# Folding a two-tile chunk into the steps of a wide chunk, with the token weights moved by another queue

## The chip, the core and the metric

One core of a Trainium2 chip runs the whole kernel. The metric is the device time of one execution in microseconds (us). Its engines are TensorE (PE in the views, with its weight loads as PEld), VectorE (DVE), ScalarE (ACT), GpSimd (POOL) and SyncE (SP), which only issues DMAs here.

## The reference

Sliding-window attention over 4 sequences of 576 tokens with 8 heads of 64, then a block that mixes tokens and then channels, then a normalised channel block. All in float32, 2304 tokens of width 512:

```python
x = attention(q, k, v)                             # window of 128, a slope for each head
h = np.maximum(x.T @ w_tok1, 0) @ w_tok2           # mixing over the 576 tokens of a sequence
u = x + h.T
u = u + np.maximum(u @ w_ch1, 0) @ w_ch2           # "layer 0": 512 -> 1536 -> 512
xn = (u - mean) / sqrt(var + 1e-6) * g_ln
out = u + np.maximum(xn @ w_ch1b, 0) @ w_ch2b      # "layer 1": 512 -> 2048 -> 512
```

## The kernel before

The 2304 tokens are 18 tiles of 128. Attention and token mixing take about the first 160 us and run in one stream of tiles; then come the two channel layers. Each float32 operand is split in a high and a low float32r part, and a product is three matmuls (high by high, high by low, low by high). The high part is a copy on ScalarE (`copy`, L385), the low part a subtraction (`minus`, L401 on VectorE, or two halves of 256 columns on GpSimd, L403).

In a channel layer the tokens go in three chunks: tiles 0 to 7 (wide, c = 0), tiles 16 and 17 (small, c = 1), and tiles 8 to 15 (wide, c = 2). In each chunk a step handles two blocks of 128 hidden channels: 6 steps to a chunk in layer 0, 8 in layer 1, so 42 steps in all. A wide step makes the first product by a scheme of seven products of half size (`seven_products`, L1122), each of 6 matmuls of 512 columns, from seven prepared forms of the transposed tokens (`prep_wide`, L902: transposes, sums, splits) and seven forms of the weights (`w1_of`, L975, through a ring of four split places, `W1_BUFS`). A small step (`two_blocks`, L1223) makes two plain blocks of 12 matmuls of 256 columns from tokens that `prep_small` (L946) has prepared. Between the products stand the units of the step before: `second` (L1236) multiplies the hidden values of a tile by the second weights, 6 matmuls of 512 columns, and VectorE adds the result to the tile (L1256). In layer 1's last chunk a faster form of it is used in all steps but the last (`second_fast`, L1261).

The prepared forms of a wide chunk lie in one place each, so the next chunk's can only be written when the present chunk's last step has read them. In the kernel before, the forms of chunk 2 are prepared piece by piece during the steps of the small chunk, and those of the next layer's chunk 0 all in the last step of chunk 2.

Weights come as float64 and are turned to float32 on the chip (`load_f64`, L411: two loads of 512 KB, one ScalarE and four VectorE operations for a tile of 256 KB). Those of layer 1 are turned ahead of need and stored in DRAM (`stage_w`, L538); how many in each step says `STAGE_RATES`. Split second weights are stored too in chunk 0 and read back by the other chunks (`w2_of`, L1037).

The first token weights are needed a second time, shifted by 64 rows, for sequences 1 and 3: `shift_wt1` (L583) copies them within SBUF by six DMAs that GpSimd issues.

The order of work on each engine is not written by hand: `Plan` (L122) records each operation with a cost, what it reads and writes, and a due time that follows from the place of TensorE's operations in the program, and schedules the list greedily. A place in a ring comes free when the planned users of its last holder are done. The engines then run that order, waiting on semaphores. SP's DMA queue is one stream in that order too.

Of the kernel before, what the change touches and what calls it, by code (L numbers as in the profile page):

```python
# [24 lines left out]
P = 128  # L25
# [17 lines left out]
W1_BUFS, W2_BUFS, ST_BUFS, H_BUFS = 4, 4, 6, 6  # L43
X_SHIFT, STAGE_SHIFT, W1_SHIFT = -20, -20, -80

STAGE_RATES = {(0, 2): 2, (1, 0): 2}
# [291 lines left out]
def block_kernel(tc, qT, kT, v, wt1, wt2, wa1, wa2, wb1, wb2, g, bias, out):  # L338
# [150 lines left out]
    for layer in range(2):  # L489
        for c, tiles in enumerate((range(8), (16, 17), range(8, 16))):  # L490
            steps += [(layer, c, tiles, n) for n in range((NF1, NF2)[layer] // 2)]
# [410 lines left out]
    def prep_wide(layer, tiles):  # L902
# [39 lines left out]
        if layer == 0 and tiles[0] == 0:  # L942
            return xs, itertools.chain(*zip(pieces(0), pieces(1)))
        return xs, itertools.chain(pieces(0), pieces(1))

    def prep_small(layer, tiles):  # L946

        out = []
        sh, sl = few()
        for j in range(2):  # L950
            b = turned(layer, [(i, 2 * j + k) for k in range(2) for i in tiles])
            copy((sh, j), lambda j=j: sh.t[:, j, :CW], b, lambda b=b: b.t, CW, ("ACT",), True)
            minus((sl, j), lambda j=j: sl.t[:, j, :CW], b, lambda b=b: b.t, (sh, j),
                  lambda j=j: sh.t[:, j, :CW].bitcast(F32), CW, ("DVE",))
# [20 lines left out]
    def w1_of(s, ahead=None):  # L975

        f1, f2 = take_w(), take_w()
        if len(steps[s][2]) == 2:
            out = [w_split("w1", W1_BUFS, x) for x in (f1, f2)]
            keep_taken(2)  # L980
            return out
# [32 lines left out]
        def others(w0, w1):  # L1014
            w2 = w_split("w1", W1_BUFS, b, all_of(b))
            w3 = w_split("w1", W1_BUFS, f2, right(f2), HW)
            keep_taken(2)
            return [(w0, 0), (w1, 0), (w2, 0), (w1, HW), (w0, HW), (w3, 0), (w2, HW)]
# [103 lines left out]
    def seven_products(ws, xs, keep, end, hid, fast):  # L1122
# [42 lines left out]
        yield  # L1165
        product(5, bb, False, end)
        out(1, 0, bb)
        yield
# [54 lines left out]
    def two_blocks(ws, xs, hid):  # L1223

        hid[0] = hidden()
        for j, (wh, wl) in enumerate(ws):
            ps = bank(2 * j)
            for k, (sh, sl, h, c) in enumerate(xs):
                s = slice(k * P, (k + 1) * P)
                mm3(ps, lambda ps=ps: ps.t[:, :HW], wh, lambda s=s, wh=wh: wh.t[:, s], wl, lambda s=s, wl=wl: wl.t[:, s],  # L1230
                    (sh, h), lambda h=h, c=c: sh.t[:, h, c], (sl, h), lambda h=h, c=c: sl.t[:, h, c],
                    HW, k == 0, k == 3)
            relu_to(hid[0], j, slice(j * HW, (j + 1) * HW), ps, lambda ps=ps: ps.t[:, :HW], HW)
            yield

    def second(s, w2, hid):  # L1236

        layer, _, tiles, n = steps[s]
        turns = list(enumerate(tiles))
        if s == len(steps) - 1:  # L1240
            turns = turns[CT:] + turns[:CT]
        for t, i in turns:
            o = buf("pst", [P, DM], F32, "tok", 2)
            if len(tiles) == 2:
                hs = [(*hid[0], j, j * HW + t * P) for j in range(2)]
# [136 lines left out]
    for _ in pieces:  # L1382
        pass

# [14 lines left out]
    for s in range(len(steps) + 1):  # L1399
# [7 lines left out]
        if len(tiles) == 2:  # L1407
            parts, ns = two_blocks(w1, xs, hid), (4, 4)
        else:
            parts = seven_products(w1, xs, keep, s == len(steps) - 1, hid, fast2(s))  # L1410
            ns = (6, 8, 0, 0) if before and fast2(before[0]) else (2, 3, 3, 0)
# [5 lines left out]
        if before and n == 0 and layer + c > 0:  # L1417
            if steps[s - 1][0] == 0:
                todo.extend((tile_stats, i) for i in steps[s - 1][2])
                todo.append((chunk_stats, steps[s - 1][2]))  # L1420
# [73 lines left out]
```

## Time and profile before

| what | value |
|---|---|
| median of 3 runs | 833.73 us (833.47 to 835.28) |
| the profiled execution | 835.53 us |
| its span, first to last instruction | 833.8 us |
| TensorE busy | 821.5 us, 4732 matmuls |
| VectorE, ScalarE, GpSimd busy | 659.1, 428.5, 466.9 us |
| moved by DMA | 179.21 MB, mean 215 GB/s |
| granted TensorE clock, mean | 0.997 of full speed |

Busy times are shares of the span in which an engine has an instruction in it. A matmul's row is longer than its turn: one of 512 columns is listed with about 390 ns, while the next starts about 227 ns later. So a short stall of TensorE leaves no idle time in the table, and the distance between starts must be read.

### The profile page before, as it was taken

To read this page: it belongs to the slowest core of one execution; us is meant where nothing else is said; L and a number is where in the kernel's file an instruction comes from. 1 tells how busy PE (TensorE), PEld (TensorE's weight loads), DVE (VectorE), ACT (ScalarE), POOL (GpSimd) and SP (SyncE) were. 2 spreads that over 40 slices of the span, in tenths; PEclk is the share of its full clock that TensorE was granted. 3 is DMA by queue.
4 is the path that set the end of the run, shared out by engine and by line. 5 is a ranking of instruction groups with operands and counts; after the bars stand their busy time and mean duration, and the time that the engine had idled before them with its cause. 6 is when DMAs were issued, how large, how long until landed. Compare 5 with 4: busy or idle time off the path is not lost.

```text
span 833.8 us, 14352 instructions
## 1 busy us (share of the span) xinstructions
PE 821.5 (99%) x4732; PEld 693.4 (83%) x4732; DVE 659.1 (79%) x1379; ACT 428.5 (51%) x1015; POOL 466.9 (56%) x723
## 2 busy tenths in 40 slices
PE   8999999999999999999999999999999999999998
PEld 6777788888888898888888888888889889999996
DVE  5888777978787989987889868989666767777785
ACT  5888677643344535334368333447456634444430
POOL 2785466756354567544248666857533656666640
PEclk9999999999999999999999999999999999999999
DMA  9679645454678899987861544888977663443302
GB/s 328 191 184 306 232 140 191 143 186 144 216 226 297 293 317 322 339 293 240 280 238 54 188 154 139 290 309 300 354 263 237 226 226 130 137 141 116 102 26 101
DMA packets 80474, 179.21 MB, mean 215 GB/s; under 512 B 9104, under 2 KB 10768, under 8 KB 80400
## 3 DMA queue, kind: packets, MB, share of 16 engines
q1 hardware_dynamic: 79920, 176.98, 62.9%
q0 software_dynamic: 480, 1.31, 0.7%
q8 instruction: 37, 0.61, 0.3%
q14 instruction: 37, 0.30, 0.1%
HBM read 138.15 MB, written 38.80 MB: 212 GB/s over the span
## 4 chain that ended last, share of the span: by engine, by line
PE 92%; DVE 4%; ACT 3%; DMA 1%; issue 1%; POOL 0%; DVEq 0%; ACTq 0%; POOLq 0%
PE tok L1253 10%; PE tok L1251 10%; PE b L1138 10%; PE tok L1252 10%; PE b L1139 10%; PE b L1140 10%; PE tok L1288 5%; PE p L1288 4%; PE ps_s L636 3%; PE ps_v L648 3%; PE p L891 2%; PE b L482 2%; PE b L481 2%; PE b L480 2%; PE ps_t L693 1%; ACT pr L686 1%
## 5 line engine op out<-in xcount | busy, mean ns | idle before, releaser
L1256 DVE TENSOR_TENSOR u<-tok,u 128x512 f32<-128x512 f32 x196 | 134.4, 687 | 52.5 <-PE tok L1253 51.1
L1251 PE MATMUL tok<-w2h,hh 128*128 128x512 f32 x392 | 154.0, 393 | 0.0
L1253 PE MATMUL tok<-w2h,hl 128*128 128x512 f32 x392 | 152.9, 390 | 0.2 <-DVE hl L971 0.2
L1252 PE MATMUL tok<-w2l,hh 128*128 128x512 f32 x392 | 152.8, 390 | 0.0
L1138 PE MATMUL b<-xh,w1h 128*128 128x512 f32 x384 | 150.4, 392 | 0.3 <-DVE b L401 0.3
L1139 PE MATMUL b<-xl,w1h 128*128 128x512 f32 x384 | 149.8, 390 | 0.0
L1140 PE MATMUL b<-xh,w1l 128*128 128x512 f32 x384 | 149.6, 389 | 0.0
L403 POOL TENSOR_TENSOR w1l<-w,w1h 128x256 fp32r<-128x256 f32 (+1 forms) x112 | 78.9, 726 | 111.4 <-ACT w1h L385 103.4
L969 ACT ACTIVATE hh<-b 128x512 fp32r<-128x512 f32 (+1 forms) x112 | 58.7, 542 | 136.8 <-PE b L1140 95.5
L1253 PEld LDWEIGHTS tok<-w2h,hl 128*128 128x128 f32 x392 | 73.6, 188 | 16.4 <-DVE hl L971 0.8
L1251 PEld LDWEIGHTS tok<-w2h,hh 128*128 128x128 f32 x392 | 73.7, 188 | 15.1 <-DVE u L1256 0.8
L971 DVE SCALAR_TENSOR_TENSOR hl<-b,hh 128x512 fp32r<-128x512 f32 (+1 forms) x112 | 67.2, 617 | 23.9 <-ACT hh L969 23.2
L1252 PEld LDWEIGHTS tok<-w2l,hh 128*128 128x128 f32 x392 | 73.7, 188 | 14.3
L1140 PEld LDWEIGHTS b<-xh,w1l 128*128 128x128 f32 x384 | 72.1, 188 | 15.4
L1138 PEld LDWEIGHTS b<-xh,w1h 128*128 128x128 f32 x384 | 72.2, 188 | 14.6 <-DVE b L401 0.7
L1139 PEld LDWEIGHTS b<-xl,w1h 128*128 128x128 f32 x384 | 72.2, 188 | 13.5
L449 ACT ACTIVATE e<-rh 128x512 bf16<-128x512 bf16 (+2 forms) x62 | 39.7, 641 | 69.4 <-DMA rh<-wb 22.2
L403 POOL TENSOR_TENSOR w1l<-st,w1h 128x256 fp32r<-128x256 f32 x58 | 44.9, 795 | 47.9 <-ACT w1h L385 42.0
L686 ACT ACTIVATE pr<-t,mn 128x128 f32<-128x128 f32 x144 | 55.8, 391 | 14.1 <-DVE mn L677 14.0
L704 POOL TENSOR_SCALAR_AFFINE_SELECT pf<-pf 128x512 f32<-128x512 f32 x64 | 42.1, 659 | 34.6 <-ACT pf L385 28.3
L401 DVE TENSOR_TENSOR b<-b,p 128x512 f32<-128x512 f32 x56 | 38.9, 695 | 20.1 <-PE b L1140 19.5
L403 POOL TENSOR_TENSOR xl<-st,xh 128x256 fp32r<-128x256 f32 x48 | 39.0, 834 | 21.0 <-ACT xh L385 16.6
(193 smaller groups left out, 1919.9 us busy)
## 6 DMA issues: line engine op xcount, KB each, us to landing
w<-d SPq DMA_DIRECT2D x86, 256.0 KB, 4.2
rw<-wb SPq DMA_DIRECT2D x32, 512.0 KB, 5.4
rh<-wb SPq DMA_DIRECT2D x32, 512.0 KB, 5.2
rw<-wa SPq DMA_DIRECT2D x24, 512.0 KB, 4.3
rh<-wa SPq DMA_DIRECT2D x24, 512.0 KB, 4.3
d<-y SPq DMA_DIRECT2D x30, 256.0 KB, 5.3
keys<-kT SPq DMA_DIRECT2D x18, 256.0 KB, 4.6
q<-qT SPq DMA_DIRECT2D x18, 256.0 KB, 4.9
```

The source lines that it names most:

```text
L403: ENGINE[e].tensor_tensor(get()[:, c], ga()[:, c], gb()[:, c], alu)
L686: op({"ACT": 580}, lambda m=m: nc.scalar.activation(out=pr.t[:, m], in_=t.t[:, m], func=AF.Exp, bias=mn.t[:, m:m + 1], scale=-1.0, accum_o ...
L969: op({"ACT": act(n, True)}, lambda: nc.scalar.activation(out=hh.t[:, c], in_=go(), func=AF.Relu), [o], [(hh, key)])
L971: mark[0] = op({"DVE": dve(n)}, lambda: nc.vector.scalar_tensor_tensor(out=hl.t[:, c], in0=go(), scalar=0.0, in1=hh.t[:, c].bitcast(F32), ...
L1138: nc.tensor.matmul(g.t, wh.t[:, w], xh.t, start=start and k == 0, stop=False, skip_group_check=True)
L1139: nc.tensor.matmul(g.t, wh.t[:, w], xl.t, start=False, stop=False, skip_group_check=True)
L1140: nc.tensor.matmul(g.t, wl.t[:, w], xh.t, start=False, stop=stop and k == 1, skip_group_check=True)
L1251: nc.tensor.matmul(o.t, hh.t[:, c:c + P], wh.t, start=j == 0, stop=False)
L1252: nc.tensor.matmul(o.t, hh.t[:, c:c + P], wl.t, start=False, stop=False)
L1253: nc.tensor.matmul(o.t, hl.t[:, c:c + P], wh.t, start=False, stop=j == 1)
L1256: op({"DVE": dve(DM)}, lambda o=o, i=i: nc.vector.tensor_tensor(u[i].t, o.t, u[i].t, ALU.add), [o], [u[i]])
L1288: nc.tensor.matmul(o.t[:, p], x()[:, c], y(), start=start and p == 0 and k == 0, stop=stop and p == 1 and k == 2, skip_group_check=True)
```

## The change

The chunks of a layer become two: tiles 2 to 9 (c = 0) and tiles 10 to 17 (c = 2). The small chunk is now tiles 0 and 1 and has no steps of its own: each step of chunk 0 also makes its two blocks (`small_block`, the body of the old `two_blocks`), one after product 6 and one after product 5, and its second products as a ninth and a tenth unit. There are 28 steps. The weights of the small blocks are the split of the first block, which the step has anyway, and that of the second block, of which the step used the right half: it is now split whole. `prep_small` takes places of its own. Chunk 2's seven forms are now prepared in the last step of chunk 0, as those of layer 1 are, and their weights' sums go ahead by the "few" places. `shift_wt1` is issued by SyncE, as float32 copies, and planned as 1820 ns of DMA instead of 3900 ns of GpSimd. The scratch for GpSimd's DMAs shrinks to 4096 bytes; 4 KB of the 12 KB gained go to a seventh pair of hidden places, 8 KB to the small chunk's tokens. The staging rates change.

```diff
-W1_BUFS, W2_BUFS, ST_BUFS, H_BUFS = 4, 4, 6, 6
+W1_BUFS, W2_BUFS, ST_BUFS, H_BUFS = 4, 4, 6, 7
+SCRATCH = 4096
+SMALL, WIDE = range(2), {0: range(2, 10), 2: range(10, 18)}
-STAGE_RATES = {(0, 2): 2, (1, 0): 2}
+STAGE_RATES = {(0, 0): 3, (0, 2): 2, (1, 0): 1}
...
-        for c, tiles in enumerate((range(8), (16, 17), range(8, 16))):
+        for c, tiles in WIDE.items():
...
-                nc.gpsimd.dma_start(out=b.t[D:], in_=a.t[:D])
-                nc.gpsimd.dma_start(out=b.t[:D, 1:], in_=a.t[D:, :4])
-                nc.gpsimd.dma_start(out=b.t[:D, 0], in_=a.t[D:, 4])
-
-            op({"POOL": 3900}, emit, [(a, k) for k in range(5)], [b])
+                x, y = a.t.bitcast(F32), b.t.bitcast(F32)
+                nc.sync.dma_start(out=y[D:], in_=x[:D])
+                nc.sync.dma_start(out=y[:D, 1:], in_=x[D:, :4])
+                nc.sync.dma_start(out=y[:D, 0], in_=x[D:, 4])
+
+            op({"DMA": 1820}, emit, [(a, k) for k in range(5)], [b])
...
-        sh, sl = few()
+        sh, sl = (buf("mlq", [P, 2, CW], F32R, f"xs{p}") for p in "hl")
...
-        if len(steps[s][2]) == 2:
-            out = [w_split("w1", W1_BUFS, x) for x in (f1, f2)]
-            keep_taken(2)
-            return out
+        whole = steps[s][1] == 0
...
-            w3 = w_split("w1", W1_BUFS, f2, right(f2), HW)
+            w3 = w_split("w1", W1_BUFS, f2) if whole else w_split("w1", W1_BUFS, f2, right(f2), HW)
...
         product(6, bd, False, end)
         out(0, 1, bd)
         yield
+        if small:
+            hid["small"] = hidden()
+            small_block(0, ws[0][0], small, hid["small"])
+            yield
         product(5, bb, False, end)
         out(1, 0, bb)
+        if small:
+            yield
+            small_block(1, ws[5][0], small, hid["small"])
         yield
...
+    def small_block(j, w, xs, h):
+
+        wh, wl = w
+        ps = bank(2 * j)
+        for k, (sh, sl, m, c) in enumerate(xs):
+            a = slice(k * P, (k + 1) * P)
+            mm3(ps, lambda: ps.t[:, :HW], wh, lambda a=a: wh.t[:, a], wl, lambda a=a: wl.t[:, a],
+                (sh, m), lambda m=m, c=c: sh.t[:, m, c], (sl, m), lambda m=m, c=c: sl.t[:, m, c], HW, k == 0, k == 3)
+        relu_to(h, j, slice(j * HW, (j + 1) * HW), ps, lambda: ps.t[:, :HW], HW)
...
-        turns = list(enumerate(tiles))
+        turns = list(enumerate([*tiles, *SMALL] if c == 0 else tiles))
...
+        if c == 0:
+            ns = (2, 3, 3, 0, 1, 1)
...
-        begun = w1_of(s + 1, "few") if end and c == 2 else None
+        begun = w1_of(s + 1, "few") if end else None
...
+            xs, pieces = prep_wide(*steps[s + 1][::2])
+            for _ in pieces:
+                pass
+            if steps[s + 1][1] == 0:
+                small = prep_small(1, SMALL)
...
-    nc = bacc.Bacc("TRN2", target_bir_lowering=False, num_devices=1)
+    nc = bacc.Bacc("TRN2", target_bir_lowering=False, num_devices=1, dynamic_dma_scratch_size=SCRATCH)
```

## Rows read from the trace of the kernel before

**Rows 1.** The page's first part: busy time, share of the span, instructions.

```profile
PE 821.5 (99%) x4732; PEld 693.4 (83%) x4732; DVE 659.1 (79%) x1379; ACT 428.5 (51%) x1015; POOL 466.9 (56%) x723
```

**Rows 2.** TensorE's waits from 140 us on: total us, times, longest.

```profile
PE tok L1288 <- DVE u L1256: 0.4, 1, 0.4
PE b L1138 <- DVE b L401: 0.3, 1, 0.3
PE tok L1253 <- DVE hl L971: 0.2, 1, 0.2
```

**Rows 3.** Timeline of TensorE in a small step: start, us, instruction.

```profile
301.10 0.28 PE L482 MATMUL b<-fewh,w1l 128*128 128x256 f32 x1
301.22 0.40 PE L1251 MATMUL tok<-w2h,hh 128*128 128x512 f32 x1
301.45 0.40 PE L1252 MATMUL tok<-w2l,hh 128*128 128x512 f32 x1
```

**Rows 4.** Timeline of TensorE around its three waits after 140 us.

```profile
330.31 0.39 PE L1140 MATMUL b<-xh,w1l 128*128 128x512 f32 x1
331.02 0.50 PE L1138 MATMUL b<-xh,w1h 128*128 128x512 f32 x1 [0.32 <-DVE b L401]
...
532.19 0.39 PE L1252 MATMUL tok<-w2l,hh 128*128 128x512 f32 x1
532.73 0.50 PE L1253 MATMUL tok<-w2h,hl 128*128 128x512 f32 x1 [0.16 <-DVE hl L971]
...
682.97 0.28 PE L1288 MATMUL tok<-w2h,hl 128*128 128x256 f32 x1
683.63 0.36 PE L1288 MATMUL tok<-rw,fewh 128*128 128x256 f32 x1 [0.38 <-DVE u L1256]
```

**Rows 5.** Groups by line: operation, shapes, count, busy us, mean ns, idle before.

```profile
L403 POOL TENSOR_TENSOR w1l<-w,w1h 128x256 fp32r<-128x256 f32 x86 | 65.5, 783 | 106.8 <-ACT w1h L385 99.4 <-issue 4.3 <-DMA rw<-wa 3.0
...
L385 ACT ACTIVATE w1h<-w 128x512 fp32r<-128x512 f32 x55 | 34.1, 624 | 5.6 <-PE b L1139 4.8 <-issue 0.7
...
L480 PE MATMUL b<-fewh,w1h 128*128 128x256 f32 x112 | 32.1, 287 | 0.0
...
L971 DVE SCALAR_TENSOR_TENSOR hl<-b,hh 128x256 fp32r<-128x256 f32 x28 | 11.7, 420 | 4.5 <-ACT hh L969 3.9
...
L969 ACT ACTIVATE hh<-b 128x256 fp32r<-128x256 f32 x28 | 10.7, 383 | 29.8 <-PE b L482 29.6
```

**Rows 6.** Stretches: busy of PE, PEld, DVE, ACT, POOL; clock, DMA share, GB/s.

```profile
160.00:284.00 124.00, 124.00 (x566) 102.97 (x565) 103.21 (x171) 54.98 (x103) 68.36 (x101) 1.00 0.62 208
...
442.00:605.00 163.00, 162.84 (x728) 134.00 (x727) 134.49 (x227) 78.80 (x157) 111.28 (x171) 1.00 0.65 225
```

**Rows 7.** Chain of waits, 317 to 332 us: start, us, what.

```profile
330.35 0.62 DVE b L401
```

**Rows 8.** Chain of waits, 438 to 458 us: its shares by line.

```profile
by line: PE tok L1253 21.0%; PE tok L1251 19.4%; PE tok L1252 19.4%; PE p L891 11.6%; PE b L1138 11.0%; PE b L1140 9.3%; PE b L1139 9.2%
```

**Rows 9.** Timeline of GpSimd, first of the shift's six issues.

```profile
53.30 0.76 POOL L587 DMA_DIRECT2D wt1h<-wt1h  x1
```

**Rows 10.** DMA from 50 to 76 us: queues; issues with KB, us to landing.

```profile
q0 software_dynamic: 480, 1.31, 23.3%
...
rh<-wt SPq DMA_DIRECT2D x2, 192.0 KB, 4.7
...
wt1l<-wt1l POOLq DMA_DIRECT2D x1, 64.0 KB, 8.6
```

**Rows 11.** TensorE's waits from 50 to 92 us that GpSimd ended.

```profile
PE tok L779 <- POOL fewl L403: 0.6, 1, 0.6
PE tok L481 <- POOL xl L403: 0.4, 1, 0.4
```

**Rows 12.** Timeline of TensorE at the first use of the shifted weights.

```profile
94.89 0.48 PE L480 MATMUL tok<-xh,wt1h 128*128 128x512 f32 x1
```

**Rows 13.** A stretch of 4 us in the attention, columns as in rows 6.

```profile
72.00:76.00 4.00, 2.62 (x17) 1.84 (x15) 2.77 (x15) 4.00 (x15) 2.74 (x6) 1.00 0.92 312
```

More of the change, by code (lines that the diff above doesn't have):

```diff
@@ L940, in pieces @@
             yield
-        if layer == 0 and tiles[0] == 0:
+        if layer == 0 and tiles == WIDE[0]:
             return xs, itertools.chain(*zip(pieces(0), pieces(1)))
@@ L1015, in others @@
             w2 = w_split("w1", W1_BUFS, b, all_of(b))
-            w3 = w_split("w1", W1_BUFS, f2, right(f2), HW)
+            w3 = w_split("w1", W1_BUFS, f2) if whole else w_split("w1", W1_BUFS, f2, right(f2), HW)
             keep_taken(2)
-            return [(w0, 0), (w1, 0), (w2, 0), (w1, HW), (w0, HW), (w3, 0), (w2, HW)]
+            return [(w0, 0), (w1, 0), (w2, 0), (w1, HW), (w0, HW), (w3, HW if whole else 0), (w2, HW)]
         if ahead == "few":
@@ L1120, in sums_of, with seven_products @@
         return w
-    def seven_products(ws, xs, keep, end, hid, fast):
+    def seven_products(ws, xs, keep, end, hid, fast, small):
         ba, bb, bc, bd = bank(0), keep[0], bank(2), keep[1]
@@ L1221, in parts_of @@
             split_h("s4", hidden())
[L1223 to L1234, printed above, removed]
+    def small_block(j, w, xs, h):
[6 more added lines that the diff above has]
+        relu_to(h, j, slice(j * HW, (j + 1) * HW), ps, lambda: ps.t[:, :HW], HW)
     def second(s, w2, hid):
-        layer, _, tiles, n = steps[s]
-        turns = list(enumerate(tiles))
+        layer, c, tiles, n = steps[s]
+        turns = list(enumerate([*tiles, *SMALL] if c == 0 else tiles))
         if s == len(steps) - 1:
@@ L1243, in second @@
             o = buf("pst", [P, DM], F32, "tok", 2)
-            if len(tiles) == 2:
-                hs = [(*hid[0], j, j * HW + t * P) for j in range(2)]
+            if i in SMALL:
+                hs = [(*hid["small"], j, j * HW + i * P) for j in range(2)]
             else:
@@ L1383, in block_kernel @@
         pass
+    small = prep_small(0, SMALL)
     todo = []
@@ L1406, in block_kernel @@
         hid = {}
[L1407 to L1411, printed above, removed]
+        parts = seven_products(w1, xs, keep, s == len(steps) - 1, hid, fast2(s), small if c == 0 else None)
+        ns = (6, 8, 0, 0) if before and fast2(before[0]) else (2, 3, 3, 0)
+        if c == 0:
+            ns = (2, 3, 3, 0, 1, 1)
         for _, k in zip(parts, ns):
@@ L1416, in block_kernel @@
             pass
[L1417 to L1420, printed above, removed]
+        if before and n == 0 and steps[s - 1][0] == 0:
+            done = steps[s - 1][2]
+            for tiles in (done, SMALL) if steps[s - 1][1] == 0 else (done,):
+                todo.extend((tile_stats, i) for i in tiles)
+                todo.append((chunk_stats, tiles))
         end = s + 1 < len(steps) and steps[s + 1][3] == 0
-        begun = w1_of(s + 1, "few") if end and c == 2 else None
+        begun = w1_of(s + 1, "few") if end else None
         pl.shift = X_SHIFT
-        if c == 1:
-            if n == 0:
-                nxt, pieces = prep_wide(layer, steps[s + (NF1, NF2)[layer] // 2][2])
-            next(pieces, None)
-            if end:
-                for _ in pieces:
-                    pass
-                xs = nxt
-        elif end:
+        if end:
             while todo:
                 do_next()
-            if c == 0:
-                xs = prep_small(layer, steps[s + 1][2])
-            else:
-                xs, pieces = prep_wide(1, steps[s + 1][2])
-                for _ in pieces:
-                    pass
+            xs, pieces = prep_wide(*steps[s + 1][::2])
[3 more added lines that the diff above has]
+                small = prep_small(1, SMALL)
         pl.shift = 0
```

6 lines of the change are left out of this document (3 added, 3 removed).

## The prediction, made before the changed kernel was run

> **What bounds the kernel now.** I read the page's busy times first. TensorE has an instruction in it for 99% of the span, VectorE for 79%, the others for less [rows 1]. That makes TensorE the suspect, but a matmul's row is longer than its turn, so the next thing to read is the distance between starts. In a small step a matmul of 256 columns starts 0.12 us before its follower and one of 512 columns 0.23 us [rows 3], although their rows last 0.28 and 0.40. Then the waits: from 140 us to the end the view of waits has just three of TensorE [rows 2]. Their true length is the distance between the starts around them less the normal one: 0.71 - 0.23 = 0.48 us at 330, 0.54 - 0.23 = 0.31 at 532, and 0.66 - 0.12 = 0.54 at 683 [rows 4]. That is 1.3 us in 690. So the two channel layers, where nearly all of the change is made, go at the pace of TensorE, and taking work off another engine gives nothing there beyond those 1.3 us. In the attention it is otherwise: between 72 and 76 us TensorE is busy for 2.62 of 4 us while ScalarE has no pause [rows 13].
>
> **The change part by part.** I make the sum against the profiled execution: 835.53 us, of which 833.8 are its span and 1.7 lie around it. That execution is 1.8 us above the median of the runs. No part below touches what lies outside the span, so I take the difference off the median, 833.73 us.
>
> *TensorE's own work.* The small steps had three groups of 112 matmuls of 256 columns [rows 5]; the new code makes 14 steps x 2 blocks x 12 = 336, the same. The second products of two tiles are 14 x 12 matmuls of 512 columns before and after, and the transposes are 18 tiles x 4 blocks x 2 layers as before. Term: 0.
>
> *Splits and reads that fall away.* The 14 small steps split two first-weight tiles each: 28 copies on ScalarE of 0.62 us and 56 half subtractions on GpSimd of 0.78 us [rows 5]. Against that, 14 steps split a whole tile in place of its half, which is less than a copy and two subtractions each. The small steps also read 56 quarter-megabyte tiles of second weights and 28 of first weights, which fall away. All of this lies behind TensorE now: in the first chunk GpSimd is busy for 68 of 124 us and DMA for 62% [rows 6]. If that cover were gone it would cost what TensorE then waited, and rows 2 show no wait on any of it. Term: 0.
>
> *More work for each step of chunk 0.* A step of chunk 0 grows by a small step's matmuls, 24 x 0.12 + 12 x 0.23 = 5.6 us [rows 3], so the 124 us of layer 0's first chunk become about 158. VectorE gets per step two additions more and two low parts of 0.42 us [rows 5], and the staged conversions. Walking the list of weights by hand, a rate of 3 makes 19 conversions in those six steps where 14 are made now; most of the staged ones are the layer's own weights, turned a little earlier. Each has four operations on VectorE; at the 0.62 us of the addition in rows 7 that is 2.5 us, an estimate. With 5 x 2.5, 12 additions and 12 low parts VectorE rises from 103 to some 128 of 158 us, 81% as against 83% [rows 6]: no more crowded. Layer 1's first chunk, where the wait at 532 falls, had VectorE busy for 134 of 163 us and GpSimd for 111 [rows 6]. It loses staging (1 for each step in place of 2, and more done before) and gets 8 x 5.6 = 45 us more to do it in. I take the wait at 532 as gone: -0.31. Bounds: gone, or still there.
>
> *The boundaries.* Preparing chunk 2 during the small steps did not keep TensorE free: the wait at 330 ends with an addition on VectorE [rows 4] and the chain there is made of that preparation, 0.62 us of it the addition itself [rows 7]. That stretch goes: -0.48. In its place come two boundaries at which the seven forms are all prepared in the last step of chunk 0. The nearest case is the present passage from layer 0 to layer 1, which does the same with the normalisation on top; its chain consists of TensorE's own rows alone [rows 8], so no wait at all. Each new boundary therefore costs between 0 and, by the wait at 330, 0.5 us. I take the middle, +0.5 for both. The wait at 683 belongs to the start of the fast form, which is as before: 0.
>
> *Order of the first chunk.* It now wants tile 9, the first tile of the third sequence, where the old one ended at tile 7. TensorE has the token mixing of the last sequence to do in the meantime. Term 0; bounds 0 and one wait like those of rows 4.
>
> *Buffers.* The seventh hidden pair covers the fifth pair that a step of chunk 0 now uses: each place is read out in the step after its writing, and with seven the place that is wanted has always been read before. With six the last output of a step would wait for the units of the same step. Term 0.
>
> *The shift.* Six DMAs leave GpSimd, of which the first holds it for 0.76 us [rows 9]; six of at most that length are under 4.6 us. What GpSimd's lateness costs TensorE there is bounded by the waits that GpSimd ends, 0.6 and 0.4 us [rows 11]. One of them comes before the shift and the other after it; I take half, -0.5, between 0 and -1.0. The shifted copy itself is not awaited: all six are issued within the 26 us of rows 10 and the slowest lands 8.6 us after its issue, so by 85 us at the latest, and the weights are first used at 94.89 us [rows 12]. On SP the six wait for the last split of the token weights, and behind them stand the loads of the second token weights and of keys, queries and values. The shift's packets take 23.3% of the 16 engines' time in 26 us, 6.1 us [rows 10]. Since a load from the queue that is already there lands in 4.7 us [rows 10] and the packets are shared out today as well, I take no loss: 0, bounds 0 and 6.1 us for what stands behind them.
>
> The Trainium skill's page "DMA: Bandwidth & Descriptors", section "Queues, rings and completion order", speaks against this part: a DMA engine takes turns between the queues that have work for it, while the descriptors within one queue are consumed in order. By that rule today's loads share with the shift, and tomorrow's stand behind it. What it would make of the sum is the fourth rival below; the row of 4.7 us, for loads beside the shift, does not contradict it.
>
> Sum: 0 + 0 - 0.31 - 0.48 + 0.5 - 0.5 = -0.8 us, so 832.9 us.
>
> **The rivals.**
>
> *A, the attention gains more.* The planner counted 7.8 us of GpSimd for the shift. Without that it orders the masks, splits and second token weights anew, and TensorE may find work in the holes, the one at 72 us being 1.4 us [rows 13]. For it: those holes are real. Against it: in that hole ScalarE is busy throughout, and it does not lose work. With both waits of rows 11 and the hole gone the shift's term is -2.4 rather than -0.5: 831.0 us.
>
> *B, all waits of the channel layers go.* The boundaries hide fully and the third wait falls away with the new order: -1.3 and 0 in place of -0.8 and +0.5, with the shift's -0.5: 831.9, and 831.4 if the shift gives its full 1.0. For it: rows 8. Against it: the fast form starts as before.
>
> *C, slower: the first weights' place comes free late.* Of the ring of four split places the first was last read by product 4, in the middle of a step. Now the first small block reads it, and only product 5, a unit, the second small block and another unit follow: 4 x about 1.4 = 5.5 us until the next step's first product wants the new split. That needs a copy of 0.62 us and two subtractions of 0.78 us, 2.2 us, on engines with queues of their own [rows 5]. The second small block's bank is tighter still: the next step's second product wants it 2.7 us later, after an activation of 0.38 and a subtraction of 0.42 us [rows 5]. If the queue ahead is too long, TensorE waits once in each of 14 steps. At 0.25 us each that is +3.5 us: 836.4. It is slower by over 0.2% from (1.7 + 0.8) / 14 = 0.18 us on. Against it: the planner orders units before a product that isn't ready, and chains as short as this end without a wait now.
>
> *D, slower: the shift stands before the loads.* If the loads of the second token weights come behind all of it on SP's queue they land up to 6.1 us later [rows 10], and the token mixing of the first sequence, which TensorE already awaits at GpSimd's part of these weights [rows 11], starts later. With half of that not refilled by other work, +3.0: 836.4 with no gain from the shift. It decides from 2.0 us of unfilled wait on.
>
> **How the numbers follow.** A change of 0.2%, 1.7 us, is about what runs of this kernel can tell from none. Chances: the sum as it stands 0.43; A 0.22 and B 0.16, both faster; C 0.13 and D 0.06, both slower. That gives faster 0.38, within 0.2% 0.43, slower 0.19. The predicted time is that of the likeliest case, 832.9 us; its own range, with the bounds of its terms, is 831.9 to 834.7. The range for all: down to 829.6, where A and B come together (-2.4 - 1.3, and the 0.3 by which the fastest run lies below the median), and up to 836.2, just below the prices of C and D as worked out, which leaves out the worse half of them and the lowest part of A with B.
>
> **What would show it.** Right: the same 4732 matmuls; starts 0.12 and 0.23 us apart; no wait of TensorE near the end of VectorE's preparation at either chunk's end that is longer than half a microsecond; the first products of chunk 0's steps following the units without a gap; GpSimd without DMA issues and the second token weights landing no later. Wrong: a wait that comes back at the start of each of the 14 steps, on the split of the first weights or on the low part of the small block; or TensorE idle for longer between 55 and 95 us, ended by a DMA; or, on the other side, far fewer holes before 95 us.

## The result, and the profile after

The changed kernel takes 839.12 us (838.90 to 840.69), the kernel before beside it 833.68 us: ratio 1.0065, 95% interval 1.0048 to 1.0083. It is slower by 5.4 us, where 832.9 was forecast and 836.2 was the upper end of the range. Three executions far above all others (4673.89 us of the kernel before, 1168.97 of the shift alone, 914.62 of the run with five places) count in no ratio below, only in the medians, and without them those two runs have 832.30 and 837.01 us.

The page's first part, busy time of each engine, answers to [rows 1]:

```profile
PE 823.2 (98%) x4732; PEld 693.1 (83%) x4732; DVE 649.4 (77%) x1374; ACT 418.3 (50%) x987; POOL 436.5 (52%) x669
```

The work went as counted: the same 4732 matmuls, VectorE 10, ScalarE 10 and GpSimd 30 us less, 161.10 MB moved in place of 179.21. Nothing of this is on the path. The view of TensorE's waits, from 160 us on, has this one line, in place of the three of [rows 2] (line waited at and releaser, us in total, times, longest):

```profile
PE b L1138 <- DVE hl L974: 3.4, 5, 1.7
```

L1138 is a high-by-high matmul of a product, here always its first one; L974 makes the low part of a hidden value. All three waits of before are gone, and one of a new kind has come. Where it is longest, the timeline of the changed kernel (start, us, instruction; in brackets the idle time before it and what ended it; a row with x4 stands for four in a row and shows the shape of the first) shows this:

```profile
630.38 0.28 PE L484 MATMUL b<-xsh,w1l 128*128 128x256 f32 x1
...
631.66 0.39 PE L1140 MATMUL b<-xh,w1l 128*128 128x512 f32 x1
632.09 1.64 ACT L972 ACTIVATE hh<-b 128x512 fp32r<-128x512 f32 x4 [3.69 <-PE b L1140]
632.72 1.62 DVE L974 SCALAR_TENSOR_TENSOR hl<-b,hh 128x512 fp32r<-128x512 f32 x3 [1.92 <-ACT hh L972]
...
633.79 0.50 PE L1138 MATMUL b<-xh,w1h 128*128 128x512 f32 x1 [1.74 <-DVE hl L974]
```

630.38 is the last matmul of a step's second small block, 631.66 the last one of that step, 633.79 the first of the next. They are 2.13 us apart, 1.90 more than the normal 0.23 [rows 3]. The line of ScalarE is the one to read. It holds four activations in a row, of 512, 256, 512 and 256 columns; the two of 256 are the small blocks'. Both blocks are done by 630.7 and ScalarE is idle for 3.69 us, yet it begins only when a product that stood behind them is done, and VectorE after it. The chain of waits says the same:

```profile
631.82 0.24 PE b L1140
632.09 0.61 ACT hh L972
632.72 1.03 DVE hl L974 x2
633.79 0.50 PE b L1138
```

Waits of this kind, by the distance between starts less the normal one, come at 184 (0.39), 318 (0.39), 498 and 525 (0.09 each), 551 (1.08), 578 (0.48) and 632 us (1.91): 4.4 us in all, each ended by a small block's low part, and each at the first product of the step that follows. Two more stand at the end of the attention, again in the timeline of the changed kernel:

```profile
132.38 0.66 PE L696 MATMUL ps_t<-ident,pr 128*128 128x128 f32 x4 [0.75 <-ACT pf L387]
133.60 0.50 PE L780 MATMUL tok<-hh,fewh 128*128 128x512 f32 x1 [0.56 <-DVE hl L757]
```

To compare kernels stage by stage I add up, for every matmul of a trace, its normal distance to the next, and take elapsed time less that sum at the moment when the sum has reached a mark. It is counted from the mark of 20 us, because executions differ in their first 20 us, as the last section shows. The mark of 120 falls at about 140 us after the start, that of 160 at about 180. What counts as normal is a choice: with the median of each line and shape whole columns come out 2 to 4 us higher, while the differences between rows stay within half a microsecond. So the rows are to be read against each other. TensorE's lost time, us:

```
sum of normal distances at         80     120     160     650     end
before                            8.6     9.5    10.2    13.5    14.6
after                             6.2     9.0    10.8    18.8    19.3
shift on SyncE alone              6.7     7.7     8.5    11.1    12.2
after, places of their own        6.2     9.0    10.8    13.7    15.1
early blocks, places of their own 6.6     7.4     8.3    10.5    11.4
```

Between 160 and 650 the changed kernel loses 8.0 us, before 3.3. That is nearly all of the difference. The third to fifth rows belong to runs below.

### The profile page after: what moved, and what is told of

It reads as the page before. It is cut to its first block, busy times and chain, and to the rows that moved or that the text cites. A ratio compares the mean times of both kernels' runs of the same rounds, so it can differ in the third digit from the quotient of the medians.

```text
span 839.0 us, 14082 instructions
## 1 busy us (share of the span) xinstructions
PE 823.2 (98%) x4732; PEld 693.1 (83%) x4732; DVE 649.4 (77%) x1374; ACT 418.3 (50%) x987; POOL 436.5 (52%) x669
## 2 busy tenths in 40 slices
DMA packets 70536, 161.10 MB, mean 192 GB/s; under 512 B 8000, under 2 KB 9664, under 8 KB 70464
## 4 chain that ended last, share of the span: by engine, by line
PE 93%; DVE 4%; ACT 2%; issue 1%; POOL 0%; DMA 0%; DVEq 0%; ACTq 0%; POOLq 0%
PE b L1138 11%; PE tok L1255 11%; PE tok L1257 11%; PE tok L1256 11%; PE b L1139 10%; PE b L1140 10%; PE tok L1292 5%; PE ps_s L639 4%; PE p L1292 4%; PE ps_v L651 3%; PE p L894 2%; PE ps_t L696 1%; PE b L484 1%; PE b L483 1%; PE b L482 1%; PE tok L483 1%
## 5 line engine op out<-in xcount | busy, mean ns | idle before, releaser
L1138 PE MATMUL b<-xh,w1h 128*128 128x512 f32 x384 | 151.7, 395 | 3.4 <-DVE hl L974 3.4
L972 ACT ACTIVATE hh<-b 128x512 fp32r<-128x512 f32 x112 | 57.1, 545 | 149.4 <-PE b L1140 127.8
L405 POOL TENSOR_TENSOR w1l<-st,w1h 128x256 fp32r<-128x256 f32 x74 | 61.0, 847 | 104.4 <-ACT w1h L387 69.7
L1138 PEld LDWEIGHTS b<-xh,w1h 128*128 128x128 f32 x384 | 72.2, 188 | 18.7 <-DVE hl L974 4.9
L974 DVE SCALAR_TENSOR_TENSOR hl<-b,hh 128x512 fp32r<-128x512 f32 x112 | 66.6, 618 | 23.9 <-ACT hh L972 23.7
L405 POOL TENSOR_TENSOR w1l<-w,w1h 128x256 fp32r<-128x256 f32 (+1 forms) x62 | 44.0, 731 | 37.8 <-ACT w1h L387 37.8
L405 POOL TENSOR_TENSOR xl<-st,xh 128x256 fp32r<-128x256 f32 x46 | 35.1, 788 | 31.0 <-ACT xh L387 31.0
```

The source lines that it names most:

```text
L405: ENGINE[e].tensor_tensor(get()[:, c], ga()[:, c], gb()[:, c], alu)
L972: op({"ACT": act(n, True)}, lambda: nc.scalar.activation(out=hh.t[:, c], in_=go(), func=AF.Relu), [o], [(hh, key)])
L974: mark[0] = op({"DVE": dve(n)}, lambda: nc.vector.scalar_tensor_tensor(out=hl.t[:, c], in0=go(), scalar=0.0, in1=hh.t[:, c].bitcast(F32), ...
L1138: nc.tensor.matmul(g.t, wh.t[:, w], xh.t, start=start and k == 0, stop=False, skip_group_check=True)
```

## The experiments

Medians are beside runs of the kernel before on the same chip (834.7 for the first four, 834.1 for the next, 833.9 for the last). The last column is the median of those executions whose mean granted clock was at least 0.999, called the full clock below; before stands at 833.5 to 833.8 there, the changed kernel at 839.0. For e5 and e8 it is a single execution.

```
run                          median  ratio to before [95%]     clock >= 0.999
e1_after_gpsimd_shift        839.66  1.0058 [1.0046, 1.0071]   838.6
e2_before_sync_shift         832.57  0.9972 [0.9962, 0.9983]   831.7
e3_five_slots                837.23  1.0033 [1.0021, 1.0044]   836.7
e4_small_early               833.66  0.9997 [0.9989, 1.0006]   833.6
e5_units_banks               839.16  1.0057 [1.0045, 1.0069]   838.9
e6_first_block_early         834.81  1.0001 [0.9992, 1.0010]   833.7
e7_early_gpsimd_shift        832.53  0.9985 [0.9975, 0.9994]   832.2
e8_units_first               859.30  1.0294 [1.0274, 1.0314]   855.9
e9_own_places                834.72  1.0011 [1.0001, 1.0021]   834.5
e10_units_first_own_places   833.62  0.9996 [0.9986, 1.0005]   833.2
e11_before_sync_own_places   835.04  1.0009 [0.9998, 1.0019]   833.3
e12_early_own_places         830.86  0.9966 [0.9953, 0.9978]   830.6
```

**The shift, undone and alone.** Two runs: the changed kernel with the shift on GpSimd again, and the kernel before with nothing changed but the shift.

```diff
-                nc.sync.dma_start(out=y[D:], in_=x[:D])
+                nc.gpsimd.dma_start(out=b.t[D:], in_=a.t[:D])
...
-            op({"DMA": 1820}, emit, [(a, k) for k in range(5)], [b])
+            op({"POOL": 3900}, emit, [(a, k) for k in range(5)], [b])
```

> The changed kernel with the shift of the token weights issued and planned on GpSimd again, all else as changed. Up to 200 us the changed kernel stands 1.3 us behind the kernel before: it gains some 2 us between 60 and 100 us and loses more at the attention's end. Theory S (the order that follows from the shift does both): the holes at 131 to 134 us go, those between 70 and 92 us come back, and the time is 837.8 us, up to 1.3 less than the changed kernel's 839.1. Rival F (the loss comes from the first wide chunk's start, tiles 2 to 9 with the small chunk's two on top): the gain goes and the loss stays, 840 to 841. Rival D of the prediction (the loads wait behind the shift): as S, but a DMA ends the waits that go.

Undoing it changes 0.5 us at most. TensorE's waits from 160 us on in that run are those of the changed kernel:

```profile
PE b L1137 <- DVE hl L973: 3.4, 5, 1.7
```

The waits at 132 and 134 us stay as well, and by the mark of 80 the run has gained as much on before as the changed kernel has, so none of the forecasts came. Neither the steps' starts nor the attention's end wait because of the shift. The second is the same diff the other way round, in the kernel before:

> The kernel before with nothing changed but the shift, issued by SyncE and planned as 1820 ns of DMA. The prediction's term: -0.5 us, 833.2. Theory S: the mixing is moved forward and the end of the attention has holes, net +1, 834.7. Rival D: a DMA ends waits of TensorE between 60 and 90 us, up to +3, 836.7.

Alone it is worth 2.1 us (0.9972), all of it made by the mark of 120 in the table above. It beats both kernels.

**Five places for the first weights.** The reason for rival C was the ring of four.

```diff
-W1_BUFS, W2_BUFS, ST_BUFS, H_BUFS = 4, 4, 6, 7
-SCRATCH = 4096
+W1_BUFS, W2_BUFS, ST_BUFS, H_BUFS = 5, 4, 6, 7
+SCRATCH = 512
```

(and 128 in place of 256 for `EVEN`, to make room).

> The changed kernel with a fifth place in the ring of split first weights, so that the next step's first split need not wait for the small blocks of this one (scratch 512 bytes, half of a padding tile left out, to make room). Theory W (the first weights' place comes free late, at the end of each step of chunk 0): the waits before the first product at 318, 551, 578 and 632 us, 3.8 us together, shrink to under 1, and the time is about 836. Rival B (the small blocks' PSUM banks, read out late by VectorE, hold the next first products): the waits stay and the time is 838.5 to 839.1.

2 us come back. The waits at 318, 551 and 578 are gone; the longest stays as it was, and TensorE's waits from 160 us on have other lines beside it (the second at the end of layer 0's chunk 0):

```profile
PE b L1138 <- DVE hl L974: 2.0, 2, 1.7
PE b L1138 <- ACT b L387: 0.6, 1, 0.6
PE b L1140 <- DVE w1l L403: 0.2, 1, 0.2
```

So the weights' place is not what the longest one awaits. I took the rest for the bank. Why a fifth place takes the other three away while the longest stays, no run shows.

**The small blocks early.** The first block behind output (0,0), the second behind output (0,1); the small tiles' units first.

```diff
         out(0, 0, ba)
+        if small:
+            hid["small"] = hidden()
+            small_block(0, ws[0][0], small, hid["small"])
         yield
...
         out(0, 1, bd)
+        if small:
+            small_block(1, ws[5][0], small, hid["small"])
         yield
...
+        if c == 0:
+            turns = turns[-2:] + turns[:-2]
...
-        if c == 0:
-            ns = (2, 3, 3, 0, 1, 1)
+        if c == 0 or before and steps[before[0]][1] == 0:
+            ns = (3, 3, 4, 0)
```

> The changed kernel with the first small block put right after product 4's output and the second after product 6's, before product 5, and the small tiles' units first among a step's units. Both the weights' place and the banks are then free a good 4 us earlier. Theories W and B: both give about 835.5, the waits at the step starts gone and 1.3 us of the first 200 us left, with the boundaries free. Rival N (it is neither; VectorE and ScalarE are simply crowded at the step starts): within 1 us of the changed kernel, 838 to 840.

All of the loss comes back, more than expected. That the blocks' place in the step matters is shown; why, it does not tell, since bank, weights' place and order of the hidden places all change with it.

**The bank by itself.** The small blocks write into the units' pair of banks.

```diff
-        ps = bank(2 * j)
+        ps = buf("pst", [P, DM], F32, "tok", 2)
```

> The changed kernel, but the two small blocks write into the pair of banks that the units use in turn, not into the banks of the first and second output. Theory bank (the next step's first product waits until VectorE has read the small block's bank): the waits at 551, 578 and above all the 1.9 us at 632, all ended by the small block's low part, go, and at most a new short wait at a unit comes; about 836, that is 3 us under the changed kernel. Rival place (what is awaited is the first weights' place in the ring of four, still read by the first small block): the waits at the steps' starts stay, ended by the split of the weights: 838.5 to 839.5. Both at work, as the run with five places let it seem: 836 to 837.5 with one kind of wait left.

The waits at the steps' starts are gone, as the theory had it, and the time is the same, as it had not: TensorE's waits from 160 us on stand elsewhere.

```profile
PE p L894 <- ACT st L886: 1.7, 1, 1.7
PE b L1138 <- ACT b L387: 1.0, 2, 0.8
```

The longest is at 655.86 us, at the end of layer 1's chunk 0: a transpose for the next chunk waits for ScalarE's normalisation (L886), and behind it the granted clock falls for a while (last section). This fits the bank as what the step's first product awaits, but the run does not tell why the bank was read out so late, nor why the normalisation is late in its order.

**Only the first block early.** As the early version, with the second block at the step's end again (`ns` = 3, 3, 4, 0, 0, 0).

> The version with the small blocks early (833.7), but the second small block back at the step's end, behind product 5; only the first one stands early, behind the first output; units of the small tiles first. The first block holds both things that the next step's first product wants, the first bank and the first weights' place; the second block holds the third bank and the sixth split, which are wanted later. Theory first block: about 833.7, within 0.7 of the version with both early. Rival second block (its late activation and low part delay what the next step wants): 836.5 to 839.

As the early version to within its interval. Either the first block's bank and weights matter, or that its hidden place is now asked for early.

**The early version with the shift on GpSimd.**

> The version with the small blocks early (833.7), with the shift back on GpSimd and planned there as in the kernel before. In the kernel before, SyncE's shift alone was worth 2.3 us; in the changed kernel undoing it changed nothing (+0.5). If the shift's gain is there whenever nothing else holds the attention's end, this run loses it: 836.0. If it was lost in the changed kernel because the fold orders the attention's end anew in a way of its own, this run stays at 833.4 to 834.2.

1.4 us faster than with SyncE at the full clock, the opposite of what it did in the kernel before. I come back to this below.

**All units before the last part.** The small blocks stay where the change put them, but no unit is left between them and the step's end.

```diff
+        if c == 0:
+            turns = turns[-2:] + turns[:-2]
...
-        if c == 0:
-            ns = (2, 3, 3, 0, 1, 1)
+        if c == 0 or before and steps[before[0]][1] == 0:
+            ns = (3, 3, 4, 0, 0, 0)
```

> The changed kernel with the small blocks where they are, but the units of a chunk-0 step all before the last part (the small tiles' units first), so that between the first small block and the next step's first product stand only product 5 and the second small block, 1.4 us each, where two units of 1.4 us stood as well. Theory (the step's start waits for the first small block's readers and what stands ahead of them on ScalarE and VectorE): each of 12 or more starts now waits, by up to 2.7 us more than before, of which the changed kernel's reserve at most starts takes a part; 1 to 2 us each, so 851 to 863, waits ended by the low part of the small block. Rival (the starts wait because engines are crowded over the whole step, not for these blocks): no more than 1 to 3 us more, 840 to 842.

20 us slower (17 at the full clock). TensorE's waits in this run from 160 us on have twelve of the kind:

```profile
PE b L1138 <- DVE hl L974: 18.9, 12, 1.8
```

The timeline around one of them:

```profile
205.10 0.28 PE L484 MATMUL b<-xsh,w1l 128*128 128x256 f32 x1
...
207.74 0.39 PE L1140 MATMUL b<-xh,w1l 128*128 128x512 f32 x1
...
208.17 1.64 ACT L972 ACTIVATE hh<-b 128x512 fp32r<-128x512 f32 x4 [1.98 <-PE b L1140]
208.80 1.95 DVE L974 SCALAR_TENSOR_TENSOR hl<-b,hh 128x512 fp32r<-128x512 f32 x4 [1.32 <-ACT hh L972]
...
209.87 0.50 PE L1138 MATMUL b<-xh,w1h 128*128 128x512 f32 x1 [1.74 <-DVE hl L974]
```

Here both small blocks are done at 205.4, two products follow, ScalarE is idle, and still the activations come in one bunch behind the last product at 208.17. ScalarE is not crowded and the blocks are not late. Something forbids it to read them.

**The hidden places named one by one.** What forbids it is in the planner. `buf` notes for each place the one recorded ahead of it in its ring, and `op` makes the first writing of a place follow the first writing of that one:

```python
        if ring:
            b.behind = ring[-1]
...
                if b.behind:
                    behind.add(b.behind.ops[0])
```

The small blocks' hidden place is recorded behind that of output (0,1). Output (0,1) needs product 6, and the planner's order has products 5 and 6 at the step's end. So the activation of the small block stands behind product 6, however early the block itself was done, and the first bank with it. The edit gives each place a ring of its own; who follows whom in a place stays the same, but the planner makes its whole order anew.

```diff
+    places = itertools.count()
+
     def hidden():
-        return [buf("hid", [P, CW], F32R, "h" + p, H_BUFS) for p in "hl"]
+        i = next(places) % H_BUFS
+        return [buf("hid", [P, CW], F32R, f"h{p}{i}", 1) for p in "hl"]
```

> The changed kernel with the seven pairs of hidden places named one by one in place of one ring of seven; the program's work, its places and who takes which after whom stay. What goes is one rule of the planner: in a ring, a place may not be written before the place recorded ahead of it has begun to be written. Theory ring order: the small blocks' place is recorded behind that of output (0,1), whose product 6 the planner puts at the step's end; so the small blocks' activations, and with them the release of the first bank, stand behind it on ScalarE. Without the rule they follow their blocks, the step starts' waits (318, 551, 578, 632) go, and the time falls to that of the early blocks or a little under: 832 to 834. Rivals bank or weights' place (the blocks simply stand too near the step's end): the waits stay, 838.5 to 839.5.

In the changed kernel this gives back 4.4 us. No wait at a step's start is left; these are TensorE's waits from 160 us on:

```profile
PE tok L1258 <- DVE u L1263: 0.4, 1, 0.4
PE b L1143 <- DVE w1l L403: 0.2, 1, 0.2
```

And ScalarE reads the small blocks when they are done. The timeline of ScalarE in the last step but one of layer 1's chunk 0, which in the changed kernel ends with the four activations at 632:

```profile
624.39 0.39 ACT L975 ACTIVATE hh<-b 128x256 fp32r<-128x256 f32 x1 [0.23 <-PE b L484]
...
627.21 0.39 ACT L975 ACTIVATE hh<-b 128x256 fp32r<-128x256 f32 x1 [0.84 <-PE b L484]
```

ScalarE's waits between 170 and 650 us tell how often an activation began as soon as a small block's last matmul (L484) was done. Of the 28 activations of small blocks, in the changed kernel it was 5:

```profile
ACT hh L972 <- PE b L484: 9.6, 5, 3.0
```

In the changed kernel with places of their own it is 22:

```profile
ACT hh L975 <- PE b L484: 33.1, 22, 3.1
```

The same edit in the version with all units first:

> The run with all units before the last part (859.3, twelve waits of 1.0 to 2.0 us at the steps' starts), with the hidden places named one by one as in the run beside it. Theory ring order: the twelve waits go although the blocks stand as late in the recorded order as they did: 833 to 838. Rivals bank or weights' place: the first bank is read only after the block at the step's end, so most of the waits stay: 850 to 860.

25.7 us come back (22.7 at the full clock) and all twelve waits are gone, with the blocks as late in the recorded order as before. TensorE's waits from 160 us on in that run are two of other kinds, the first at the end of layer 1's chunk 0:

```profile
PE p L897 <- DVE st L403: 0.9, 1, 0.9
PE p L1297 <- ACT p L1311: 0.7, 1, 0.7
```

The same edit in the kernel before with the shift on SyncE:

> The kernel before with the shift on SyncE (832.6, 2.3 us under the kernel before) and the six pairs of hidden places named one by one. Before has no small block behind an output of the same step, so the ring's order should hold up nothing there: 832.0 to 833.2, the same as with the ring. If the ring's order costs something in every chunk, not only where the small blocks were put, it falls by 1 us or more, to 831.5 or less. It is also the fair partner of the changed kernel with places of their own: the difference of the two is what the fold itself is worth without the ring's order.

It does not help there, it costs 1.6 us at the full clock, and the forecast of no change was wrong. By the marks, the attention is as in the run with the ring (7.8 at 120), and the loss lies between 300 and 500 us. TensorE's waits of that run from 160 us on are two new ones:

```profile
PE p L895 <- ACT st L887: 1.1, 1, 1.1
PE b L1144 <- DVE w1l L401: 0.7, 1, 0.7
```

So the ring's order was no cost that shows in the kernel before, and a new order of the planner alone can move the time by 1.6 us or more. The 4.4 us of the changed kernel are therefore not exact; what carries the cause are the seven waits that go there and the twelve that go in the version without units at the step's end. Last, the edit in the early version:

> The version with the small blocks early (833.7), with the hidden places named one by one. Its small blocks' place is recorded second in the step, ahead of the late outputs, so theory ring order has little left to take: its waits at 362 and 653 (0.6 and 0.8 us) may go, 832.0 to 833.7, and within 0.7 us of the changed kernel with places of their own, since the planner is then free to choose the same order for both. If early blocks helped by their place and not by the ring's order, this run is 2 us or more under the changed kernel with places of their own.

830.86 us, 0.9966 of the kernel before: the fastest of all, and below what was forecast. One wait of TensorE is left in the view from 160 us on:

```profile
PE tok L1260 <- DVE hl L977: 0.2, 1, 0.2
```

It is 3.9 us under the changed kernel with places of their own, which was to speak for early blocks helping by their place in the step. The table of lost time speaks against that: of 3.7 us, 2.5 lie before the mark of 160, all of it ahead of the first small block (at 174 us), and 1.2 behind it.

## Why the prediction was wrong

**The step that failed is the paragraph on the buffers, with its term of 0.** It asked whether a place is free when it is wanted, and with seven pairs it is. It did not ask in which order a ring's places may be begun. That order holds the small blocks' activations behind a later product, the first bank is read out late, and TensorE waits at the next step's start. It costs 4.4 us by the clock (839.12 to 834.72) and 5.1 us between the marks of 160 and 650 (8.0 to 2.9), of which 4.4 are the seven waits and the rest the slower matmul behind each (its row lasts 0.50 at 633.79, 0.39 to 0.40 in [rows 3] and [rows 4], and its follower starts 0.11 us later than normal). The two lines of the planner quoted above were to be read, and the diff calls `hidden()` between two outputs.

**Rival C named the place and the sign, not the cause.** It had 0.13, TensorE waiting at the start of each step of chunk 0, 836.4. The waits come there, in 7 steps rather than 14, 0.1 to 1.9 us each rather than 0.25. The sign that the prediction named for it came, a wait on the low part of the small block. But it put them down to the weights' ring of four or to a bank read late by a chain that is too long. The bank is indeed read late, but by the ring's order: with four places, the same banks and the same chain, the waits go when that order goes. Its argument against itself, that the planner fills in before a product that isn't ready, is what hides most of the starts; the version without units there shows what it hides, 12 waits and 18.9 us.

**TensorE's own work: 0.** Right, 4732 matmuls and the same distances.

**Splits and reads that fall away: 0.** Right. 30 us of GpSimd and 18 MB went and bought nothing.

**More work for each step, -0.31, and the boundaries, -0.48 + 0.5.** The waits at 330, 532 and 683 went. The new boundaries cost the changed kernel nothing of their own, nor its version and the early version with places of their own. That is luck of the planner's order in part: by the distance between starts, the run with all units first and places of their own waits 1.0 us there (at 654.82), and the one with the units' banks 1.0 (at 363.64) and 1.9 us (at 655.86), more than the 0.5 us that was the bound. From 160 to 650 the version with places of their own loses 2.9 us against 3.3 before, so -0.4 where the sum had -0.3.

**Order of the first chunk: 0.** Between the marks of 120 and 160 the changed kernel loses 1.8 us, before 0.7: +1.1, beyond the bound of one wait like those of [rows 4] (0.3 to 0.5 us). It stays with places of their own, and is nearly gone in the early version with places of their own (0.9).

**The shift, -0.5.** The sign was right where it was tried alone, and the size not: -2.1, near rival A's -2.4. But it is no price that could be added. At the full clock, SyncE's shift against GpSimd's is worth -2.1 us in the kernel before, +0.4 in the changed kernel, which the runs can't tell from nothing, and +1.4 in the early version, where the intervals of the two ratios just overlap. Each time the planner orders the attention anew. At the mark of 80 the changed kernel had gained 2.4 us on before, which it keeps with GpSimd's shift and so does not owe to SyncE's, and lost 1.9 again by 120, most of it in the two waits at 132 and 134. These stand in the changed kernel, in the runs with GpSimd's shift and with five places, and in the one with places of their own, not in the others. What in the recorded order brings them about I have not settled. That the changed kernel stands 0.5 us ahead of before at the mark of 120, as the term had it, is luck.

**Rival D, the shift ahead of the loads.** The Trainium skill, page "DMA: Bandwidth & Descriptors", section "Queues, rings and completion order", has the descriptors of one queue consumed in order on each DMA engine. Rival D made of it that the loads behind the shift wait. The view of DMA issues from 50 to 76 us of the changed kernel (KB each, median us to landing) shows no loss against before:

```profile
v<-v SPq DMA_DIRECT2D x5, 256.0 KB, 4.1
keys<-kT SPq DMA_DIRECT2D x4, 256.0 KB, 5.0
...
rh<-wt SPq DMA_DIRECT2D x2, 192.0 KB, 4.3
...
wt1l<-wt1l SPq DMA_DIRECT2D x1, 320.0 KB, 5.1
...
wt1l<-wt1l SPq DMA_DIRECT2D x1, 64.0 KB, 6.9
```

`rh<-wt` lands in 4.3 us where it took 4.7 [rows 10], the last part of the shift in 6.9 where it took 8.6. The medians hide something of the rule: one by one, the two loads of `wt` issued right behind the shift, at 57.35 and 59.21 us, land after 5.9 and 5.2 us, the three issued from 62.75 to 65.83 after 2.9 to 4.1. Before, loads issued beside the shift took up to 8.7. So being behind it costs less here than sharing with it did. Rival D is out: the run with the shift alone gained.

**What the fold is worth.** All at the full clock: the kernel before with SyncE's shift has 831.7, the fold in its best form 830.6, and as changed but without the ring's order 834.5, where its partner with the same edit has 833.3. So the fold comes out 1.1 us ahead in the first pair and 1.2 behind in the second, less than a new order alone has moved, and the best form is the best of several while its partner is one run. The intervals of the two best (0.9962 to 0.9983 and 0.9953 to 0.9978) overlap. No worth of the fold by itself is shown, as the argument that TensorE sets the pace had it.

**The range.** Its lower end is by its own terms 829.7 (833.73 - 2.4 - 1.3 - 0.3) and not 829.6, which changes nothing.

## What to carry to other kernels

Where a planner hands out places from a ring, read the ring's order of first use as a dependency like any other: a block inserted between two outputs stands behind whatever the first output waits for, however early it is done. An engine that is idle beside finished work, and then runs it in one bunch behind something else, is the sign of such a dependency; a late bank or buffer is only where it shows. Two runs with one edit, in the version that hides the wait and in one that lays it bare, settled with two numbers (4.4 us, and 25.7 or at the full clock 22.7) what four runs on the suspected resources could not. And in a kernel that a greedy planner orders, a small edit's worth is not a constant: the same shift was worth -2.1 us in one version and, by medians at the full clock, +0.4 and +1.4 in two others, and a mere reordering cost 1.6.

## What the hardware showed besides

In most kernels here the executions fall into two groups, 1.4 to 2.0 us apart: the medians are 833.5 and 835.2 for the kernel before (beside the last four runs) and 830.6 and 832.6 for the fastest. The second has a mean granted clock of 0.997 to 0.998, the first 0.999 to 1.000. The windows view, with columns as in [rows 6], shows where they part. First the profiled execution of before:

```profile
10.00:12.00 2.00, 0.95 (x7) 0.47 (x5) 1.73 (x10) 1.83 (x10) 0.24 (x1) 1.00 1.06 405
12.00:16.00 4.00, 3.49 (x16) 2.76 (x18) 2.25 (x10) 2.25 (x12) 1.50 (x3) 0.58 1.04 401
```

Then the same stretches of before with SyncE's shift:

```profile
10.00:12.00 2.00, 1.31 (x10) 0.84 (x8) 1.80 (x12) 1.91 (x9) 0.24 (x1) 1.00 1.06 405
12.00:16.00 4.00, 3.12 (x31) 2.46 (x32) 3.29 (x11) 2.52 (x15) 1.48 (x3) 1.00 1.04 398
```

And of the early version with places of their own:

```profile
10.00:12.00 2.00, 1.31 (x10) 0.84 (x8) 1.80 (x12) 1.93 (x9) 0.24 (x1) 1.00 1.06 397
12.00:16.00 4.00, 3.12 (x19) 2.53 (x20) 2.82 (x10) 2.88 (x15) 1.48 (x3) 0.75 1.04 399
```

In the first and the third the granted clock of the 4 us is 0.58 and 0.75 of full speed, so for a part of them it is at the lower level of 1.2 GHz, and 16 and 19 matmuls are made; in the second it stays at 2.4 GHz and 31 are made. TensorE's work just before does not tell which it will be: the second and the third have the same 1.31 us of 2. What decides it, no run here shows. Of the fourteen traces, the clock falls there in eight. The first 20 us of matmuls take 1.2 us longer for it (9.8 of lost time in before against 8.6 with SyncE's shift), whatever the kernel does later.

The clock can fall later too. The run with the small blocks in the units' banks keeps it in the first 20 us, and loses it behind its longest wait:

```profile
654.00:656.00 2.00, 0.28 (x3) 0.14 (x1) 1.28 (x2) 2.00 (x5) 1.93 (x3) 1.00 0.00 0
656.00:662.00 6.00, 5.86 (x22) 4.39 (x22) 4.24 (x8) 6.00 (x15) 2.31 (x4) 0.72 0.00 0
```

In this execution the wait and the slower matmuls behind it take 4.2 us more than normal, about as much as the steps' starts had cost. The run's one execution with a mean granted clock of 1.000 is only 0.3 us faster, so how its time adds up stays open. The changed kernel's wait of the same length at 632 us brings no such fall in its trace, where the granted clock from 634 to 638 us is 1.00. A single execution's span therefore says nothing on a change of 1.7 us here before its clock is read.
